# Building half of the float64 weight chunks with one VectorE operation fewer, and sending four more attention tiles through the DMA transpose

## The chip, the cores and the metric

The kernel runs on one core of one Trainium2 chip. The metric is the device time of the one launch in microseconds (us), as the median of three runs. Beside it one execution was recorded by the hardware profiler; its rows are what this text reads.

The engines are called as in the profile: PE (TensorE matmul), PEld (its weight load, which overlaps PE), DVE (VectorE), ACT (ScalarE), POOL (GpSimd) and SP (SyncE, which here only issues DMAs).

## The reference

Clustered attention, then two dense blocks. A query sees only the keys of its own cluster; the cluster is the centroid with the largest normalised product.

```python
q_assign = argmax(einsum('bhsd,hcd->bhsc', q_n, c_n)); k_assign = argmax(... k_n ...)
mask   = q_assign[:, :, :, None] == k_assign[:, :, None, :]
scores = where(mask, D ** -0.5 * q @ k.T, -1e9)
x      = softmax(scores) @ v                       # B=2, H=8, S=768, D=64
h = x @ w_in                                       # 1536 x 512 @ 512 x 2048
g = where(h >= 1, h, where(h <= -1, 0, (h + 1) ** 2 / 4))
x = g @ w_out                                      # 2048 x 512
out = (((x @ w1) * (x @ w2)) @ w3) @ w_out2        # 512 -> 1024 -> 1024 -> 512
```

q, k, v and the centroids are float32. All weights are float64: each arrives as two 32-bit words, and the kernel makes float32 of them on the chip.

## The kernel before

**Attention.** The 2 batches x 4 pairs of heads are 8 units. A unit has 2 groups of 384 queries, a group 6 tiles (2 heads x 3 blocks of 128 queries), so there are 96 tiles `s`, 48 in each batch. A tile goes through: four matmuls into a 128x768 score tile in PSUM (`s_mm`, L853), the row maximum on DVE (L861), a small operation on POOL that turns it into the bias (L866), the exponential on ACT (L874), a transpose, and, when the six tiles of a group are there, the product with v (`pv`, L962 in batch 0, L970 in batch 1).

**The two ways to transpose.** `by_pe(s)` picks one. Where it holds, ACT writes the exponential to SBUF, PE turns it in six 128x128 transposes back into the score tile's PSUM (`s_pT`, L891), and ACT and DVE copy it to `pt`. Where it doesn't, ACT and DVE split the tile into two 16-bit halves in `phl` (L347, L352), and SP issues one DMA transpose from `phl` to `pt` (L921). In batch 0 every tile goes by PE; in batch 1 every sixth, which is 8 of 48.

**Weight chunks.** The float64 weights come in 72 chunks of 128x512 (`chunk`). ACT takes the absolute value of the high word read as a float (L1107); DVE clamps it (L1111, sometimes POOL), shifts its bits left by three (`rebase`, L1117) and puts the two top bits back (`top`, L1123). The low word's upper three bits are then added: in even chunks ACT scales them (L1136) and POOL adds (L1140), in odd chunks DVE shifts and ors (`low`, L1129). Chunks are used at once or stored to DRAM and loaded again.

**Dense blocks.** Weights and activations are split into a high and a low part, and each product is three matmul passes (`mm4`, L1254: 12 matmuls of 384 columns). w3 @ w_out2 is multiplied in advance (`wp_mm`, L1198). Batch 0's dense work runs between the attention tiles of batch 1; batch 1's comes last, most of it in a form with seven products in place of eight (L1507).

**What sets the order.** Nothing is scheduled at run time or while building. All tasks are listed with `add`, and a long string, `ORDER`, names each task and the engine that does it, in the order in which they are issued. Every engine works through its own part of that list in order and waits at each instruction for what it needs. At the start 40 matmuls that compute nothing (`idle_mm`, L463) stand between the first tiles on PE.

Of the kernel before, what the change touches and what calls it, by code (L numbers as in the profile page):

```python
# [8 lines left out]
F32 = mybir.dt.float32  # L9
# [4 lines left out]
U32 = mybir.dt.uint32  # L14
# [24 lines left out]
    "##$V$.$0$4#%#*$X$2#,#0$]#.$Z%s%X%V%Z#(%e#2#4%h%k$6%c$_%y&,%r:m%_$H$8%m$::|$a;.$<%a;<$q%|$c$>%i#_$J&%#i#e$e%u"  # L39
    "&#%]$s#:$@$g$D#Z:o$L$i#o$k:w#N#6:q#>$B$m$##q#c$F#T:s#D;H$N#k&($,:u)u;#$u:y#y%o$()w#|;0#J#H%w#]$o$*$%;%#B)y)|"  # L40
    "#s$P;(;>$R$w*#;X;*#g*%#F$y#P#L;R;,#w$|*($T;2**;g;J;8;4*,*4%#&*;L*.*@;@;6;Z*6;:*B;i*0;q*8*:;k#a*D*L;B#u;u*F;D"
    ";m*<#R;F*2*H;o*>#8;]#@;s*N<(#m*X*Z*J#<*P*R#X#V*u;_*];a;w*_;N;y+(;c*T*V*e;e;P*a*c+4;|;T<**w*m&>&0+6*y*g<6+*<2"
    "+8<B<,*|+,<.+:&3+#+.&9+L<#<R+0+%&7<%*i+2+@<0*k+X+N<e<4<8+<<D+B;V+>*o+D<T+P<F+R<V+Z+F*r+]<u<X+H<H&:<Z+_+T<J+J"
    "+a&G+e+u*s+g&/+V+c,(<g&=,4<L+m,*&4<N<w+w%@<o,6+y,,+|<:,8<i,.<<,@,:<>,#<y<|,<,%<@,0<]<k,L,2<_<P=*,B=:,N,>,D,F"
    ",P=#=%,R&I=(,X<a,H<m<c,u,J<q+i=L,w-4+k&J,Z,y=,<s-6,]=],|+o-8=.=k,_=0=2&N=4,T,W&D-#=6,e=<&T,a-(&Q,g=N=8,c-*-%"
    "=>-,+r=_=|+s-.=a=@&@-:=P=B-@=D-<&B=R-0=F=V=c=T,m&_=H-B=X&Z-2-D>4->=e=g&L&S=i>D&W-L=J=m-F-X=p&c,i-N&k-u&X,l-H"
    "-Z&o=Z&j>R-]=u=q-P-_=s-R-K=w,o-a>#-w>6-T=y>%-V-y>(,q>*-|>,>.-c>8,s%>&e>F>T>H>:>>.(><&].#.*>]-m>V.%.,>X>c>u>Z"
    ">0>J..&b>L-e.0&g>N-g.4>P.@%B>@.6%(-i%%.L-k>_>2.2>B.N?%.B.P.8.:.<-o.D&u&n.F>e>w.H?,.X>z.R>a.Z.J>g?:?J.].>>i._"
# [36 lines left out]
    "[]Zw^.[iZy]u[m^:[k_;[|],]#[(]q]._=^<]%`D^>]0]([*_>^2]*]g^@Z|^6]3_C[,]s^D_6]w_8`F[_]4_G_@^L]e[o^B^H]i]6^R_I]8"
# [54 lines left out]
def cluster_attention_moe_kernel(  # L140
# [947 lines left out]
    def low_by_pool(i):  # L1088
        return i % 2 == 0
# [683 lines left out]
```

## Time and profile before

| | |
|---|---|
| time, median of 3 runs | 726.48 us (725.79 to 728.29) |
| profiled execution | 725.32 us, of it 723.6 us span |
| instructions | 11965 |
| HBM read, written | 73.70 MB, 20.19 MB |

The span runs from the first to the last instruction; the 1.72 us beyond it lie around it. An engine's busy share is a mean over stages that differ: attention of batch 0 up to about 210 us, attention of batch 1 with the dense work of batch 0 up to about 470 us, then dense work alone. The ends of matmuls are modelled, so that short gaps on PE don't show as idle time; the starts of consecutive matmuls tell more.

### The profile page before, as it was taken

The numbers are of one execution on the slowest core, as the hardware profiler recorded it, in microseconds if no ns is written. First come the engines' busy times: TensorE is split into PE (matmuls) and PEld (weight loads), VectorE is DVE, ScalarE is ACT, GpSimd is POOL, SyncE is SP. The second block draws the span as 40 slices with busy tenths as digits, with TensorE's granted clock in tenths as the row PEclk, the third lists the DMA queues.
The fourth block names the chain that finished last, engine by engine and source line by source line (L and its number), as shares of the span: only waits on it lengthen the run. The fifth ranks groups of instructions, "written<-read, shape, count | busy, mean of one in ns | idle before, by whom it ended". The sixth has DMA issues, their size and how long they took to land.

```text
span 723.6 us, 11965 instructions
## 1 busy us (share of the span) xinstructions
PE 704.4 (97%) x4144; PEld 617.9 (85%) x4145; DVE 615.9 (85%) x1134; ACT 465.5 (64%) x870; POOL 285.3 (39%) x358
## 2 busy tenths in 40 slices
PE   5899999999999999999999999999999999999998
PEld 2766666566599999999999999999999999999997
DVE  6998988988987898999999998749987888999851
ACT  7888987766878678788778675425764534454301
POOL 4232325222245343345444525421762432377501
PEclk9999999999999999999999999999999999999999
DMA  8453658656788879888989887854131221122212
GB/s 312 135 193 131 194 192 272 202 191 201 205 166 199 171 175 217 233 235 187 244 217 225 205 230 157 186 164 152 46 103 57 59 88 59 44 72 74 73 52 80
DMA packets 113932, 115.80 MB, mean 160 GB/s; under 512 B 74128, under 2 KB 82768, under 8 KB 113872
## 3 DMA queue, kind: packets, MB, share of 16 engines
q1 hardware_dynamic: 91312, 55.62, 31.8%
q10 hardware_dynamic: 22560, 59.42, 26.6%
q8 instruction: 32, 0.52, 0.3%
q14 instruction: 28, 0.23, 0.1%
HBM read 73.70 MB, written 20.19 MB: 130 GB/s over the span
## 4 chain that ended last, share of the span: by engine, by line
PE 89%; DVE 4%; ACT 3%; DMA 2%; issue 1%; SPq 0%; POOL 0%; ACTq 0%; POOLq 0%; DVEq 0%
PE mo L1254 36%; PE sc L1507 9%; PE sc L853 9%; PE mo L1198 7%; PE mo L1507 5%; PE sc L891 5%; PE sc L1254 5%; PE av L962 4%; PE av L970 3%; PE av L1507 2%; PE av L1254 2%; DMA vn<-phl 1%; DMA kq<-in_qT_dram 1%; DVE nm L861 1%; ACT pt L347 1%
## 5 line engine op out<-in xcount | busy, mean ns | idle before, releaser
L1254 PE MATMUL mo<-X,whl 128*128 128x384 f32 x924 | 169.5, 338 | 0.0
L1254 PEld LDWEIGHTS mo<-X,whl 128*128 128x128 f32 x924 | 159.5, 188 | 2.3 <-issue 0.6
L1254 PE MATMUL mo<-G,whl 128*128 128x384 f32 x732 | 133.2, 337 | 0.0
L1254 PEld LDWEIGHTS mo<-G,whl 128*128 128x128 f32 x732 | 126.6, 188 | 0.9 <-DVE X L352 0.3
L861 DVE TENSOR_REDUCE nm<-sc 128x1 f32<-128x768 f32 x96 | 90.2, 952 | 15.9 <-PE sc L853 13.6
L352 POOL TENSOR_TENSOR whl<-wf,whl 128x512 fp32r<-128x512 f32 x48 | 63.3, 1319 | 73.1 <-ACT whl L347 44.6
L1140 POOL TENSOR_TENSOR wf<-wf,w 128x512 int32<-128x512 int32 x32 | 42.2, 1320 | 80.4 <-DVE wf L1123 32.1
L866 POOL TENSOR_SCALAR nm<-nm 128x1 f32<-128x1 f32 x96 | 26.3, 274 | 102.9 <-DVE nm L861 94.2
L347 ACT ACTIVATE whl<-wf 128x512 fp32r<-128x512 f32 x76 | 47.5, 627 | 29.4 <-PE mo L1254 11.8
L853 PE MATMUL sc<-k,q 128*128 128x512 f32 (+1 forms) x192 | 55.1, 368 | 3.8 <-DVE nm L861 1.6
L1198 PE MATMUL mo<-wo,wf 128*128 128x512 f32 x128 | 58.0, 596 | 0.0
L874 ACT ACTIVATE P<-sc,nm 128x768 f32<-128x768 f32 x56 | 50.1, 898 | 10.6 <-POOL nm L866 5.5
L347 ACT ACTIVATE pt<-sc 128x768 f32<-128x768 f32 (+1 forms) x50 | 39.4, 807 | 18.6 <-PE sc L891 14.7
L853 PE MATMUL sc<-kq 80*128 80x512 f32 (+1 forms) x192 | 49.7, 340 | 0.0
L891 PEld LDWEIGHTS sc<-ident,P 128*128 128x128 f32 x336 | 37.9, 141 | 12.5 <-issue 4.9
L1107 ACT ACTIVATE wf<-w 128x512 f32<-128x512 f32 x64 | 42.4, 672 | 5.7 <-POOL wf L1140 1.7
L891 PE MATMUL sc<-ident,P 128*128 128x128 f32 x336 | 43.9, 275 | 1.6 <-DVE nm L861 1.3
L1123 DVE SCALAR_TENSOR_TENSOR wf<-w,wf 128x512 uint32<-128x512 uint32 x64 | 44.2, 693 | 0.9
L874 ACT ACTIVATE sc<-sc,nm 128x768 f32<-128x768 f32 x40 | 34.7, 868 | 15.5 <-POOL nm L866 15.4
L1198 PEld LDWEIGHTS mo<-wo,wf 128*128 128x128 f32 x128 | 23.3, 190 | 24.5 <-issue 23.7
L352 DVE TENSOR_TENSOR phl<-sc,phl 128x768 f16<-128x768 f32 x40 | 38.1, 952 | 5.6 <-ACT phl L347 5.2
L853 PEld LDWEIGHTS sc<-k,q 128*128 128x128 f32 x192 | 31.4, 189 | 12.2 <-DVE nm L861 3.0
(239 smaller groups left out, 1485.1 us busy)
## 6 DMA issues: line engine op xcount, KB each, us to landing
wf<-wd ACTq DMA_DIRECT2D x64, 256.0 KB, 2.7
w<-in_w_out_dram ACTq DMA_DIRECT2D x24, 512.0 KB, 4.2
wd<-wf SPq DMA_DIRECT2D x48, 256.0 KB, 3.6
w<-in_w3T_dram ACTq DMA_DIRECT2D x16, 512.0 KB, 4.7
w<-in_w_in_dram ACTq DMA_DIRECT2D x16, 512.0 KB, 5.0
w<-in_w_dram ACTq DMA_DIRECT2D x16, 512.0 KB, 4.3
wf<-wp ACTq DMA_DIRECT2D x16, 256.0 KB, 2.9
kq<-in_qT_dram SPq DMA_DIRECT2D x8, 384.0 KB, 3.4
```

Source lines behind the costliest of these rows:

```text
L347: nc.scalar.activation(out=out, in_=in_, func=AF.Copy)
L352: (nc.gpsimd if e == "POOL" else nc.vector).tensor_tensor(out=out, in0=a, in1=b, op=ALU.subtract)
L853: nc.tensor.matmul(ps[:, n], q[0:n_rows, q0:q0 + 128], k[0:n_rows, n], start=first, stop=not first)
L861: nc.vector.tensor_reduce(out=nm, in_=T[("sc", b), s], axis=AX.X, op=ALU.max, negate=True)
L874: nc.scalar.activation(out=new(("P", b), s).rearrange("p n s -> p (n s)") if by_pe(s) else T[("sc", b), s], in_=T[("sc", b), s], func=AF.E ...
L891: nc.tensor.transpose(T[("sc", b), s][:, c], p[:, c], ident)
L1107: nc.scalar.activation(out=T["wf", i], in_=T[w64, i].bitcast(F32)[:, :, 1], func=AF.Abs)
L1123: nc.vector.scalar_tensor_tensor(out=w, in0=T[w64, i][:, :, 1], scalar=0xC0000000, in1=w, op0=ALU.bitwise_and, op1=ALU.bitwise_or)
L1140: nc.gpsimd.tensor_tensor(out=w, in0=w, in1=T[w64, i].bitcast(I32)[:, :, 0], op=ALU.add)
L1198: nc.tensor.matmul(acc, w[:, k4 * 128:(k4 + 1) * 128], wo2[:, hf * 4 + k4], start=(hf == 0 and k4 == 0), stop=(hf == 1 and k4 == 3),)
L1254: nc.tensor.matmul(acc, w[:, a, k4 * 128:(k4 + 1) * 128], rhs(c, k4), start=(first and k4 == 0 and n == 0), stop=(last and k4 == 3 and n = ...
L1507: nc.tensor.matmul(ps, lhs(av, a, k), rhs(bv, c, k), start=k == 0 and n == 0, stop=k == 1 and n == 2,)
```

## The change

`PE_EVERY` goes from (1, 6) to (1, 12): of the 48 tiles of batch 1 now 4 are turned by PE. Tiles 54, 66, 78 and 90 take the way over `phl` and the DMA transpose.

The 36 odd chunks are put together in another way. ACT's absolute value also multiplies by 2^16, which does what `rebase` did by masking; a new ACT operation (`low_floor`) scales the low word and rounds it down to its upper three bits; one DVE operation shifts and ors these in (`shift_low`) and another puts the sign back (`sign`). That is clamp, shift_low, sign in place of clamp, rebase, top, low on DVE, and one ACT operation more. The even chunks stay as they are.

`ORDER` is a new string: all engines' lists change, and some tasks change engine. Counted over the whole program, 44 DMA transposes become 48 and PE has 24 matmuls fewer; DVE has 36 two-operand scalings fewer but 33 copies and casts more and 11 subtractions or additions fewer; ACT has two activations more in all; POOL has 12 additions or subtractions more.

```diff
-    "##$V$.$0$4#%#*$X$2#,#0$]#.$Z%s%X%V%Z#(%e#2#4%h%k$6%c$_%y&,%r:m%_$H$8%m$::|$a;.$<%a;<$q%|$c$>%i#_$J&%#i#e$e%u"
+    "###%$V$.$2$0#*#,#0$X$4$]$Z%s%X%Z#.:m%V#(#2%c#4$6%r%e%k$_$H%|%h:|&#&%$8$:$a%y%_&,#m#L;.%]$<$>$q$c%m$@$J$D$e$F"
...
-    PE_EVERY = (1, 6)
+    PE_EVERY = (1, 12)
...
+        nc.gpsimd.memset(down, -0.4982)
...
+        by_add = low_by_pool(i)
...
-            nc.scalar.activation(out=T["wf", i], in_=T[w64, i].bitcast(F32)[:, :, 1], func=AF.Abs)
+            nc.scalar.activation(out=T["wf", i], in_=T[w64, i].bitcast(F32)[:, :, 1], func=AF.Abs, scale=1.0 if by_add else float(2.0 ** 16))
...
-                out=w, in0=w, scalar1=float(2.0 ** -15), scalar2=float(2.0 ** 16 * 1.875), op0=ALU.max, op1=ALU.min
+                out=w, in0=w, scalar1=float(x * 2.0 ** -15), scalar2=float(x * 2.0 ** 16 * 1.875), op0=ALU.max, op1=ALU.min
+        def low_floor(e):
+            lo = T[w64, i][:, :, 0]
+            nc.scalar.activation(out=lo, in_=lo, func=AF.Identity, scale=float(2.0 ** -29 - 2.0 ** -41), bias=down)
+
+        def shift_low(e):
+            w = T["wf", i].bitcast(U32)
+            nc.vector.scalar_tensor_tensor(
+                out=w, in0=w, scalar=3, in1=T[w64, i][:, :, 0], op0=ALU.logical_shift_left, op1=ALU.bitwise_or
+            )
+
+        def sign(e):
+            w = T["wf", i].bitcast(U32)
+            nc.vector.scalar_tensor_tensor(
+                out=w, in0=T[w64, i][:, :, 1], scalar=0x80000000, in1=w, op0=ALU.bitwise_and, op1=ALU.bitwise_or
             )
...
-        def low(e):
-            w = T["wf", i].bitcast(U32)
-            nc.vector.scalar_tensor_tensor(
-                out=w, in0=T[w64, i][:, :, 0], scalar=29, in1=w,
-                op0=ALU.logical_shift_right, op1=ALU.bitwise_or,
-            )
...
-                add(("wc", i, 3), {"DVE": 0.6}, t - 7.0, low, [("wc", i, 2)], frees=[(w64, i)])
+                add(("wr", i), {"ACT": 0.56}, t - 8.5, low_floor, [("wl", i), "c_const"])
+                add(("wc", i, 2), {"DVE": 0.6}, t - 7.8, shift_low, [("wc", i, 0), ("wr", i)])
+                add(("wc", i, 3), {"DVE": 0.6}, t - 7.0, sign, [("wc", i, 2)], frees=[(w64, i)])
```

**Place 1: PE around tile 54,** the first tile of batch 1 that changes its way. `sc` rows with `k,q` and `kq` are the four matmuls of one tile's scores, `whl` rows are twelve matmuls of the dense block, `ident,P` the six transposes. Before:

```order
L1254 MATMUL mo_123<-X_75,whl 128x384 x12
L853 MATMUL sc_1736<-k_97,q_100 128x512
L853 MATMUL sc_1736<-k_97,q_100 128x256
L853 MATMUL sc_1736<-kq_103 128x512
L853 MATMUL sc_1736<-kq_103 128x256
L1254 MATMUL mo_1730<-X_75,whl 128x384 x12
L891 MATMUL sc_1735<-ident,P_106 128x128 x6
L1254 MATMUL mo_1731<-X_75,whl 128x384 x12
```

And now:

```order
L1268 MATMUL mo_124<-X_75,whl 128x384 x12
L855 MATMUL sc_1736<-k_98,q_101 128x512
L855 MATMUL sc_1736<-k_98,q_101 128x256
L855 MATMUL sc_1736<-kq_104 128x512
L855 MATMUL sc_1736<-kq_104 128x256
L1268 MATMUL mo_1730<-X_75,whl 128x384 x12
L1268 MATMUL mo_1731<-X_75,whl 128x384 x12
```

The six transposes are gone and the dense products on both sides follow each other; the same happens at tiles 66, 78 and 90. The rest of PE's list keeps its pattern, with neighbours exchanged here and there.

**Place 2: DVE at the first odd chunk.** `wo` is the chunk's float32, `w` its two words; `phl` rows belong to the cluster masks. Before:

```order
L1111 TENSOR_SCALAR wo_118<-wo_118 128x512
L567 STREAM_TRANSPOSE phl_109<-phl_109 128x384
L1117 TENSOR_SCALAR wo_118<-wo_118 128x512
L562 TENSOR_TENSOR phl_110<-P_107,amx 128x384
L1123 SCALAR_TENSOR_TENSOR wo_118<-w_112,wo_118 128x512
L567 STREAM_TRANSPOSE phl_110<-phl_110 128x384
L1129 SCALAR_TENSOR_TENSOR wo_118<-w_112,wo_118 128x512
```

And now:

```order
L564 TENSOR_TENSOR phl_111<-P_108,amx 128x384
L569 STREAM_TRANSPOSE phl_110<-phl_110 128x384
L1114 TENSOR_SCALAR wo_119<-wo_119 128x512
L569 STREAM_TRANSPOSE phl_111<-phl_111 128x384
L1124 SCALAR_TENSOR_TENSOR wo_119<-wo_119,w_113 128x512
L1130 SCALAR_TENSOR_TENSOR wo_119<-w_113,wo_119 128x512
```

Four rows of the chunk became three: the short one (L1117) is gone, the two long ones stay as long ones, and the mask's rows moved ahead of the chunk.

**Place 3: PE in its first 20 us.** `kq,cT` rows are the products with the centroids, four for each half of k or q; `ident` into `av` are matmuls that compute nothing; `raw` is the transpose of v; `tri` the cluster masks. Before:

```order
L533 MATMUL sc_178<-kq_117,cT 32x384 x8
L463 MATMUL av<-ident 128x128 x3
L783 MATMUL sc_177<-ident,raw_91 128x128 x6
L463 MATMUL av<-ident 128x128
L574 LDWEIGHTS tri
L574 MATMUL sc_177<-phl_109,tri 128x384
```

And now:

```order
L535 MATMUL sc_179<-kq_118,cT 32x384 x4
L465 MATMUL av<-ident 128x128 x2
L535 MATMUL sc_179<-kq_118,cT 32x384 x4
L576 LDWEIGHTS tri
L576 MATMUL sc_178<-phl_110,tri 128x384
L465 MATMUL av<-ident 128x128 x4
L785 MATMUL sc_178<-ident,raw_92 128x128 x6
```

The first mask product moved ahead of v's transpose, and two of the idle matmuls went between the two halves of the centroid products. There are 40 idle matmuls in both programs, all ahead of tile 6.

## Rows read from the trace of the kernel before

**Rows 1.** The page's busy time by engine: us, share of span, instructions.
```profile
PE 704.4 (97%) x4144; PEld 617.9 (85%) x4145; DVE 615.9 (85%) x1134; ACT 465.5 (64%) x870; POOL 285.3 (39%) x358
```

**Rows 2.** Busy time by stage: length, then us and count by engine.
```profile
core 0: us, PE busy (x) PEld busy (x) DVE busy (x) ACT busy (x) POOL busy (x), PEclk, DMA share, GB/s
0.00:15.00 15.00, 6.81 (x36) 1.69 (x37) 8.56 (x25) 12.75 (x16) 8.20 (x15) 1.00 0.85 306
15.00:30.00 15.00, 12.16 (x93) 10.86 (x92) 13.75 (x29) 10.84 (x18) 2.54 (x4) 1.00 0.58 190
30.00:42.00 12.00, 9.97 (x70) 8.56 (x68) 10.79 (x21) 10.48 (x20) 4.27 (x7) 1.00 0.34 112
42.00:60.00 18.00, 17.75 (x103) 11.42 (x103) 17.21 (x29) 15.88 (x28) 4.97 (x11) 1.00 0.50 173
60.00:210.00 150.00, 149.01 (x778) 94.16 (x776) 132.54 (x217) 116.61 (x200) 48.51 (x72) 1.00 0.64 201
210.00:450.00 240.00, 238.53 (x1509) 223.89 (x1508) 220.35 (x381) 181.01 (x334) 103.35 (x122) 1.00 0.89 208
450.00:690.00 240.00, 240.00 (x1395) 237.47 (x1394) 202.66 (x419) 114.53 (x252) 109.58 (x128) 1.00 0.32 91
690.00:723.60 33.60, 30.16 (x174) 29.84 (x173) 10.00 (x19) 3.41 (x7) 3.89 (x3) 1.00 0.18 63
```

**Rows 3.** PE in order of time around a transposed tile: start, us, what.
```profile
225.15 0.82 PE L891 MATMUL sc<-ident,P 128*128 128x128 f32 x6
225.73 2.35 PE L1254 MATMUL mo<-X,whl 128*128 128x384 f32 x12
227.92 0.57 PE L853 MATMUL sc<-k,q 128*128 128x512 f32 x2
...
228.67 2.25 PE L1254 MATMUL mo<-G,whl 128*128 128x384 f32 x12
230.76 0.51 PE L1254 MATMUL mo<-X,whl 128*128 128x384 f32 x2
```

**Rows 4.** DVE and ACT groups of the chunks: busy us, mean ns.
```profile
L1117 DVE TENSOR_SCALAR wf<-wf 128x512 uint32<-128x512 uint32 x64 | 28.6, 452 | 0.8
L1123 DVE SCALAR_TENSOR_TENSOR wf<-w,wf 128x512 uint32<-128x512 uint32 x64 | 44.2, 693 | 0.9
L1129 DVE SCALAR_TENSOR_TENSOR wf<-w,wf 128x512 uint32<-128x512 uint32 x32 | 23.5, 735 | 0.6
L1136 ACT ACTIVATE w<-w 128x512 uint32<-128x512 uint32 x36 | 24.3, 674 | 1.5 <-POOL wf L1140 1.1 <-DMA w<-in_w3T_dram 0.4
```

**Rows 5.** ACT over 384 columns from PSUM, with and without a pointer bias.
```profile
L1262 ACT ACTIVATE tmp<-mo,half 128x384 f32<-128x384 f32 x32 | 18.4, 574 | 7.4 <-PE mo L1254 7.2
L347 ACT ACTIVATE tmp<-mo 128x384 f32<-128x384 f32 x24 | 11.6, 487 | 38.6 <-PE mo L1254 37.2 <-DVE whl L352 0.9 <-DVE wf L1129 0.4
```

**Rows 6.** What PE waited for: us in total, times, longest.
```profile
PE av L439 <- DVE P L435: 5.8, 1, 5.8
PE sc L533 <- DMA kq<-in_qT_dram: 1.9, 2, 1.4
PE sc L853 <- DVE nm L861: 1.6, 2, 1.1
PE sc L853 <- DVE phl L352: 1.5, 2, 0.8
```

**Rows 7.** PE in order of time, where it waited for ACT at 41 us.
```profile
41.34 0.62 PE L853 MATMUL sc<-k,q 128*128 128x256 f32 x2 [0.24 <-ACT pt L347]
```

**Rows 8.** Transposes of group 4,1 on SP, its product on PE; transposes' landing.
```profile
247.81 3.66 SPq L921 DMA_TRANSPOSE pt<-phl  x2
...
260.46 3.12 PE L970 MATMUL av<-pt,vn 128*64 128x384 f16 x36
...
DMA to landing us min/median/max: 3.6/5.2/10.2
```

More of the change, by code (lines that the diff above doesn't have):

```diff
@@ L44 @@
[L44 to L48, printed above, removed]
@@ L94 @@
[L94 to L95 removed]
+    "###%$V$.$2$0#*#,#0$X$4$]$Z%s%X%Z#.:m%V#(#2%c#4$6%r%e%k$_$H%|%h:|&#&%$8$:$a%y%_&,#m#L;.%]$<$>$q$c%m$@$J$D$e$F"
+    "%a#6#a#e#P;<%u:o$s$g#Z$i$B$L$k#F;H%i:q%o$m:s)u$N:w:u%w#:$#:y#V#H#8;#;()w#g#c$o$u#_#i#@#X;0#y)y)|;8#u#w$w#B*#"
+    "#q;X*%$P;%#>$y$|;*;,;2;R;>$R$T*(**#R#o;g#]*4*,%#&*;B;4*.;_&)$,#T;6;@;:*6;J*@*B#s$%;Z*0;i*8#N*:;L;N*L#|;k*D*F"
@@ new lines @@
+    "*<;D#k;m*2;F*>*H#<;]#J#D*N;u;q*X;o*P*J$($**Z;a*R*]*u<(*_+(*T;P;T;w;c;e*a*W;|*c*e*g+4*w<6*m<*;s<B+*<2&0*y+6+,"
+    "*|&5&3<R&>+.;y<,+8+:<.<#+L+#<8<%+0<<+<+%<:&7*i+2+@<0*k<D+X+B<4;V<T+N<e+D<X*o+P+F+Z+R*r+]&/+_+H+T*s+>&=+J+V+u"
+    "+a+e<V<><F<H+c,4&:<Z,(+w&8<g+m,*+y<u<o<@,,+|,6<i<J,8,:,#<],.<k<_,L<L<N<m,&=*&F<|,0,<,@+g<P,B=:<q<w,N,2,P<y,>"
+    "=#=%,D,R,X&H=L<b,F<c,u,w=,=(+i+k%>=.,Z,H,T=]%%<s,]%(,y=0=4=2=@=6,_,|,a,K,W=V-#+o=<=N=>=B-4&c=Q-(+r-%=k,c=8-*"
+    "-,-6&D=c=|=_+s-8-:=D=a=e-.=R&U-@&@&B=F-0-<=g=i=I,e&L,m-2-B-D=J&N-?&K,g-F,i&R&Y=u=T&W>(=m-H-X,l=X,o=o-L-K&P&_"
@@ new lines @@
+    "-N-P-Z=Z>4>D>R-R-],r=q=s&e-_&^-u=w>>%B>#-w-T-a&b-y>c-V>%=y>J>*-|.#,s>6-d>,>8>F>T>.-e.(>]-g>:-m.*>u.%&k>H.,>L"
+    "..>N>V>X><>0&g-i&[>2>@.4%*>P.@-l.L.6%@?,>Z.8>i.0>B.B.D.:.N>_.2&n&r.P&i.F.<.R&u-o>e?%.X.Z.H>a>w.]?:>y>|._&p?#"
+    "?(-q.J?J.>>q.T.V>g>k>m>s.u.a?2/4.w?.>o/(&y?0?*?]/6.c.y.|&|/*(%()?m/,&w/@/#/./0($(-?P?D-s?<?4%,.m%D/B?>?L?_?@"
+    "/8/:/<?a?6.e?8.g?N?R/%%./2?T/>?c?V?B%F%0?o?s?|%2?g/D?F?H/F/H@2?q%4(*?e%H?i%J?X/L?u/J?Z.i/N/X@D.k&s%L/P?k@,/Z"
+    "/R/T%6/]?w%N@#/_?y@T(.@&.o.r%8/a/V/c%P.s@c@8%:@(/u@*@4/m%<%R%T@.@F@V@s/w/y/e(4@6@:@N0(@<04@H/|0#@JA,@>0608@Z"
@@ new lines @@
+    "0@@L@00*0:0,@P0&0B0.000D@m0<@A/g/i0F0LA<0H@X@]@e03@_0X/k@g@a@B0N@R0>@i0P0J0Z/o@kAJ0R0]0u@yA60T0w@u@o@qA.@w0y"
+    "A>@|0|/r0_AB0a0WA#A%A@ALAD0cAFAH(01(/s(20eA0AZ1#1L0g1*0m1,1.10ANAP1NA2AT1%ARAVA4A(A*(612A81416180iF4FP1@Aa0l"
+    "1X(81:1PA:1Z1B1]1_1D0o(;1<(=1FA]1H1RAmA_AX(>Ac1J(EAe(BAg1>(A1e1g(M(H1TAi0q1a1W(NAk1i1c2*(GAo0sB21kAq1u2,(J1m"
+    "BP1w2.201y1|(P(Z22(RB424B61o2#2%1r1s26(T2(Bo(VAsAuAw(X282:BRBTB%B(Ay2F(]B82<2H2JC42>2A2LBc2BB+B,B:A|B=2DBr2N"
+    "BDB#2PCRCqBeB>2RBg2TB/B1C7F>BsC(C9BFBiFkB@BH2cBB2V2XBV2eBJ2g2ZC*BM2]2_C-BuBk2iBNCU2aBm2kC.BXCV3%3(2mBZBw3*D%"
@@ L96 @@
+    "e(fBeifDe*e%g@f|f?e]fHeQe_gigke,emg$g*g.g%eqf6fJfPeog2esg(gNgmekeuewfWg4fLeygpfNfZf]fFgqg0h4g6g8g:h_f_gyfRfX"
+    "gthae|gFgBh#g~h&fcg-gvgxfTh)fgfih*fegDfahBfkhghihcfmfoh8hFgPiTh6h<gHfqh,heh0hogRhsg<hkh2gTgXi*huhDg]h:gVhmiW"
+    "gJi,h.h>hHiXi_g`gahwi8iqh~gZi#i.hNi:hzh@hJi2iagci<isicgfi]i%hLhqggi0hPi|i>ivhRi4hTj4hXh[i)iwi@iDhViHiJiZi6iL"
+    "j>iBh]iFiNiyj$iQieiRikj&j(igjPiij6jAj9imjCj.j0j2jSjUj<jVj:jJjXjZjLj*j,j^j`iojNjDjgjjjGjkjHjajcje"
 )
@@ L194, in cluster_attention_moe_kernel @@
     nbig = const.tile([128, 1], F32, name="nbig")
+    down = const.tile([128, 1], F32, name="down")
     wp = dram.tile([DM // 128, 128, KF2, 128], F32, name="wp")
@@ L1162, in chunk @@
             add(("wc", i, 0), {"DVE": 0.34, "POOL": (1.92, LATE)}, t - 8.6, clamp, [("wabs", i)])
-            add(("wc", i, 1), {"DVE": 0.34}, t - 8.2, rebase, [("wc", i, 0)])
-            add(("wc", i, 2), {"DVE": 0.6}, t - 7.8, top, [("wc", i, 1)])
-            if low_by_pool(i):
+            if by_add:
+                add(("wc", i, 1), {"DVE": 0.34}, t - 8.2, rebase, [("wc", i, 0)])
+                add(("wc", i, 2), {"DVE": 0.6}, t - 7.8, top, [("wc", i, 1)])
                 add(("wr", i), {"ACT": 0.56}, t - 8.5, low_round, [("wl", i)])
```

89 lines of the change are left out of this document (37 added, 52 removed).

## The prediction

> **What bounds the kernel now.** I read the busy time by engine first, then the busy time by stage, then what PE waited for. PE is busy 704.4 us of 723.6, DVE 615.9 [rows 1]. By stage the picture is sharper [rows 2]. Up to 42 us PE stands idle for 8.19, 2.84 and 2.03 us in the three stretches, 13.06 in all; from 42 to 690 us it is idle for 0.25 + 0.99 + 1.47 + 0 = 2.71; in the last stretch, which ends with the last copy and store, for 3.44. So from 42 us on the time is the length of PE's own list. DVE is the next, 220.35 of 240 us between 210 and 450, but PE hardly waits for it: the list of PE's waits has eleven rows, the largest are the first centroid transpose (5.8) and the first loads (1.9), and the waits for the row maximum and for the 16-bit low half are 1.6 and 1.5 [rows 6]. A change pays here if it shortens PE's list or one of the waits up to 42 us, and it costs if it puts a wait into the stretch after that. The granted clock is 1.00 in every stage, so no term of it is in the sum.
>
> **Four tiles leave PE.** What one costs PE is read from the starts around one of them [rows 3]. From the first of its six transposes (225.15) over the twelve dense matmuls behind it to the next instruction (227.92) are 2.77 us; twelve dense matmuls without transposes in front take 230.76 - 228.67 = 2.09. One tile is 0.68 us, four are 2.72. It comes from the stage between 210 and 450 us, where PE is 99.4% busy and dense products stand on both sides of the gap, ready to close it, as the first place in the order shows. I count it in full: -2.72.
>
> The same tiles get what the other 40 of batch 1 have. ACT and DVE make their two halves as before (into `phl`, not `pt`), which is no new operation on either. SP gets four DMA transposes; two take it 3.66 us, one 1.83 [rows 8]. SP is in order, so the stores and loads behind wait that much longer. The transpose itself lands after 5.2 us (median; 3.6 to 10.2), and then the product of the group may start. For the group that holds tile 54 the last two transposes are issued from 247.81 on, the second from about 249.64, and the product starts at 260.46, 10.8 us later [rows 8]. A sixth transpose ahead of it leaves 9.0 us, still over the median landing. From below the cost is 0, from above it is what a landing beyond 9.0 us takes from PE (10.2 would be 1.2). I take 0, since the median is far inside.
>
> The Trainium skill (VectorE: DVE Perf Modes, "The three transpose paths" and "Rules for kernel authors") speaks against this: it gives 390 ns for a 128x128 transpose on TensorE and 1309 ns by DMA, and advises TensorE where the result may lie in PSUM. By its figures six blocks cost 2.3 us on one and 7.9 us on the other (an estimate from that page), so four tiles would lose 22 us if somebody waited for them. The rows show 0.68 us for the one, 5.2 for the other, and nobody waiting for the 5.2; by them the rule holds for the latency and not for the engine that sets the end.
>
> **Chunks on DVE and ACT.** Each of the 36 odd chunks loses one DVE operation, the short one: 0.452 us [rows 4], 16.3 in all. The two that stay long are bounded by the two rows of the same form, 0.693 and 0.735; the sum over both is the same as before, so 0 for them. ACT gets 36 operations. The even chunks' scaling has 0.674 us; the new one has a pointer bias, which in another ACT form makes 574 of 487 ns, 87 more [rows 5]; so 0.674 to 0.761 each, and I take the upper, 27.4 us. ACT has that room: it is busy 10.84 of 15, 10.48 of 12, 15.88 of 18, 116.61 of 150 and 181.01 of 240 us [rows 2], 100 us idle up to 450. It doesn't get them in full anyway: the new order gives DVE 33 copies and casts that ACT had, and POOL 12 subtractions that DVE had. The freed DVE time is mostly spent on that.
>
> What is it worth on PE? After 42 us at most the 2.71 us that PE idles there; and since DVE's list has hardly become shorter I take nothing of it. Before 42 us the order lets me bound it. Ahead of the ninth tile's maximum, three rebases (chunks 1, 3, 5) are gone on DVE, 1.36 us, and one tile's copy came in that ACT had; ahead of the sixth tile's copy ACT has three new operations, 2.28 us. ACT is idle for 4.16 + 1.52 us between 15 and 42 [rows 2], which hides them if they fall into its gaps; at 41 us PE waited 0.24 us for ACT [rows 7], so the cover there is thin. So the start is between -1.4 (DVE's gain in full) and +2.3 (ACT's load in full). I take 0, between the two. The mask product that moved ahead on PE (third place) can't start before DVE has made its input, and v's transpose behind it loses nothing; 0.
>
> **Sum.** -2.72 on the profiled execution's 725.32 is 722.60. The median of the runs is 726.48, 1.16 above it, so the forecast in the terms of the median is 723.76, that is 723.8 us: -0.37%.
>
> **Rivals.**
> 1. *The start gets shorter too.* DVE's 1.36 us and the earlier mask reach PE, and some of the 2.71 us of idle time go: -2.72 - 2 = 721.8. For it: DVE is busy 13.75 of 15 and 10.79 of 12 us there, and PE waits for it. Against: the order fills DVE again.
> 2. *The start gives it back.* The three new ACT operations ahead of the first product delay the copies that PE waits for, by 2.28 us, and nothing after 42 us can catch up, since PE has no slack there: -2.72 + 2.28 = -0.44, 726.0. For it: the wait at 41 us. Against: ACT's 5.7 us of gaps.
> 3. *A transpose comes late, slower than before.* Between 210 and 450 us the DMA engines are busy to 0.89 [rows 2]. If one more transpose in that crowd makes the longest landing longer by a median one, 10.2 + 5.2 = 15.4 us, the product of tile 54's group waits 15.4 - 9.0 = 6.4 us; PE is in order, and all that stands behind waits with it: -2.72 + 6.4 = +3.7, 730.2. It decides from a landing of 9.0 us on, and is slower than before by more than the bound from 13.9 on. That is what the rule of the Trainium skill on transposes (VectorE: DVE Perf Modes, "Rules for kernel authors") would come to in this kernel. Against it: PE waited for no product in the trace, with 40 tiles on that way.
> 4. *The new order alone.* With every list changed, waits may appear anywhere. I give it no own time; it widens the forecast's own range to about 1.3 us on either side.
>
> **How the numbers follow.** The forecast gets 0.52, the first rival 0.19, the second 0.20, the third 0.09. A measurement of this kernel can tell about 0.3% from no change, 2.2 us, so faster is below 724.3 and slower above 728.7. Of the forecast's 0.52 about seven in ten lie below 724.3, 0.37, and the rest within; the first rival is faster, the second within, the third slower. Faster 0.37 + 0.19 = 0.56, same 0.15 + 0.20 = 0.35, slower 0.09. The range takes in the first rival down to -2.72 - 1.4 - 1.5 = 720.9 and the second with the upper bounds of start and landing together, -2.72 + 2.28 + 1.2 = 727.2; it leaves out the third and the ends of the others. The forecast's own range is 722.5 to 725.1.
>
> **What would show it.** PE's busy time falls by about 2.7 us, with 24 transposes fewer. PE's idle time up to 42 us stays near 13 us and after it near 2.7. DVE's group of the masked shift has half its count. The new ACT group has 36 entries of 0.67 to 0.77 us. No row of PE's waits names a product. It would be wrong if PE's waits grow by more than 2 us anywhere, first of all for ACT's copies before 42 us, or if a product waits for a transpose.

## The result, and the profile after

The changed kernel takes 732.61 us (median of 16 runs, 728.30 to 734.91); the kernel before took 725.84 in the same comparison (16 runs, 724.35 to 729.39). The ratio is 1.0083 with a 95% interval of 1.0064 to 1.0101: about 6.1 us slower (4.6 to 7.3), where 2.7 us less were forecast. The time lies outside the forecast's range.

The profiled execution took 729.0 us, 727.3 of it span. It is one of the faster of its runs: its mean granted clock is 1.000, while 10 of the other 15 had 0.995 or less. What these have more is seen in a second trace below.

The page of the changed kernel, busy time by engine as in [rows 1]:

```profile
PE 706.3 (97%) x4120; PEld 620.5 (85%) x4121; DVE 620.3 (85%) x1120; ACT 467.9 (64%) x872; POOL 308.2 (42%) x371
```

PE has the 24 instructions fewer, and is busy 1.9 us longer. DVE has not become shorter (615.9 before), as the prediction said: the new order fills it again.

Busy time by stage, columns as in [rows 2]:

```profile
0.00:15.00 15.00, 6.21 (x37) 2.38 (x37) 10.03 (x23) 11.80 (x15) 7.36 (x16) 1.00 0.85 306
15.00:30.00 15.00, 11.65 (x89) 10.26 (x86) 14.16 (x28) 11.28 (x19) 3.44 (x4) 1.00 0.56 190
30.00:42.00 12.00, 10.22 (x72) 8.73 (x70) 11.00 (x20) 10.99 (x21) 4.60 (x6) 1.00 0.36 114
42.00:60.00 18.00, 17.92 (x101) 11.84 (x103) 17.22 (x32) 16.59 (x29) 4.57 (x9) 1.00 0.41 141
60.00:210.00 150.00, 147.96 (x774) 92.81 (x772) 133.00 (x211) 115.80 (x202) 56.18 (x74) 1.00 0.66 211
210.00:450.00 240.00, 238.49 (x1485) 223.57 (x1484) 218.13 (x369) 184.78 (x339) 113.08 (x126) 1.00 0.89 206
450.00:690.00 240.00, 239.96 (x1385) 237.38 (x1384) 204.32 (x421) 112.44 (x245) 119.00 (x137) 1.00 0.32 93
690.00:727.30 37.30, 33.85 (x192) 33.53 (x190) 12.49 (x25) 4.20 (x9) 0.00 (x0) 1.00 0.21 71
```

PE is idle 13.92 us up to 42 us (13.06 before) and 3.67 from 42 to 690 (2.71 before). That is 1.8 us of the 3.7 by which the two profiled spans differ. The rest hides in rows that look full: between 450 and 690 us PE is busy for all of the 240 us in both kernels, with 1395 instructions before and 1385 now. The same list takes longer there.

The durations of the chunks' operations are near what [rows 4] and [rows 5] gave. The rows that answer to them (`L1120` is the new ACT operation, `L1124` and `L1130` are the two that stay on DVE):

```profile
L1120 ACT ACTIVATE w<-w,down 128x512 uint32<-128x512 uint32 x36 | 27.7, 770 | 3.4 <-POOL wf L1152 2.3 <-ACT P L876 0.6 <-issue 0.5
L1130 DVE SCALAR_TENSOR_TENSOR wf<-w,wf 128x512 uint32<-128x512 uint32 x32 | 23.2, 725 | 0.4
L1124 DVE SCALAR_TENSOR_TENSOR wf<-wf,w 128x512 uint32<-128x512 uint32 x32 | 23.2, 724 | 0.9
```

What PE waited for, columns as in [rows 6]:

```profile
PE av L441 <- DVE P L437: 7.4, 1, 7.4
...
PE mo L1268 <- DVE X L353: 0.8, 1, 0.8
PE mo L950 <- DVE wf L350: 0.7, 1, 0.7
```

The first row was 5.8. The other two weren't in the list of before. No row names a product.

### The profile page after: what moved, and what is told of

Read it like the earlier page. It is cut to its first block, busy times and chain, and to the rows that moved or that the text cites. A ratio compares the mean times of both kernels' runs of the same rounds, so it can differ in the third digit from the quotient of the medians.

```text
span 727.3 us, 11952 instructions
## 1 busy us (share of the span) xinstructions
PE 706.3 (97%) x4120; PEld 620.5 (85%) x4121; DVE 620.3 (85%) x1120; ACT 467.9 (64%) x872; POOL 308.2 (42%) x371
## 4 chain that ended last, share of the span: by engine, by line
PE 86%; DVE 5%; DMA 4%; ACT 3%; issue 2%; POOL 0%; ACTq 0%; POOLq 0%; DVEq 0%
PE mo L1268 34%; PE sc L1521 9%; PE sc L855 8%; PE mo L1212 6%; PE sc L1268 6%; PE mo L1521 6%; PE sc L893 4%; PE av L964 4%; PE av L972 3%; PE av L1521 2%; PE av L1268 2%; DMA vn<-phl 1%; DMA pt<-phl 1%; DMA wd<-wf 1%; DVE nm L863 1%
## 5 line engine op out<-in xcount | busy, mean ns | idle before, releaser
L1268 PE MATMUL mo<-G,whl 128*128 128x384 f32 x696 | 129.1, 340 | 0.8 <-DVE X L353 0.8
L1268 PEld LDWEIGHTS mo<-G,whl 128*128 128x128 f32 x696 | 122.3, 188 | 2.8 <-DVE X L353 1.1
L1152 POOL TENSOR_TENSOR wf<-wf,w 128x512 int32<-128x512 int32 x32 | 45.0, 1408 | 56.9 <-DVE wf L1142 18.1
L868 POOL TENSOR_SCALAR nm<-nm 128x1 f32<-128x1 f32 x96 | 29.7, 310 | 92.0 <-DVE nm L863 88.7
L348 ACT ACTIVATE whl<-wf 128x512 fp32r<-128x512 f32 x71 | 44.6, 628 | 29.0 <-PE mo L1268 10.0
L876 ACT ACTIVATE sc<-sc,nm 128x768 f32<-128x768 f32 x44 | 38.3, 870 | 26.4 <-POOL nm L868 25.3
L876 ACT ACTIVATE P<-sc,nm 128x768 f32<-128x768 f32 x52 | 46.4, 896 | 13.0 <-DVE nm L863 7.0
L353 DVE TENSOR_TENSOR phl<-sc,phl 128x768 f16<-128x768 f32 x44 | 41.8, 951 | 8.2 <-ACT phl L348 7.9
L353 POOL TENSOR_TENSOR wh<-ws,wh 128x256 fp32r<-128x256 f32 x42 | 31.3, 758 | 17.8 <-DVE wh L350 9.6
L348 ACT ACTIVATE pt<-sc 128x768 f32<-128x768 f32 (+1 forms) x40 | 31.8, 811 | 9.7 <-PE sc L893 7.4
```

The source lines that it names most:

```text
L348: nc.scalar.activation(out=out, in_=in_, func=AF.Copy)
L353: (nc.gpsimd if e == "POOL" else nc.vector).tensor_tensor(out=out, in0=a, in1=b, op=ALU.subtract)
L868: nc.gpsimd.tensor_scalar(out=tl[s, "nm"], in0=tl[s, "nm"], scalar1=SCALE, scalar2=EC, op0=ALU.mult, op1=ALU.add)
L876: nc.scalar.activation(out=new(("P", b), s).rearrange("p n s -> p (n s)") if by_pe(s) else T[("sc", b), s], in_=T[("sc", b), s], func=AF.E ...
L1152: nc.gpsimd.tensor_tensor(out=w, in0=w, in1=T[w64, i].bitcast(I32)[:, :, 0], op=ALU.add)
L1268: nc.tensor.matmul(acc, w[:, a, k4 * 128:(k4 + 1) * 128], rhs(c, k4), start=(first and k4 == 0 and n == 0), stop=(last and k4 == 3 and n = ...
```

## The experiments

Each group of runs was made on one chip, beside runs of the kernel before on that chip; between groups the ratios are compared. "No shift" means that the new constant lies in a second column of the constant 0.5, so that no other tile in SBUF moves.

### 1. The changed kernel again, and three neighbours

**The changed kernel once more.** No edit.

> The changed kernel once more, as the measure for the three beside it, and for a second trace. Both theories expect the 1.008 of the first comparison again, some 6 us over before. Theory 'clock': if a part of the loss is PE at half clock, the mean granted clock of this trace is below 1.00 (the first comparison listed 0.995 for most runs, which over 730 us is about 7 us at half clock, 3.6 us lost), and a window of the trace shows where. Theory 'no clock': the trace reads 1.00 like the first, and the time still is near 732.

732.86 us, ratio 1.0103 (1.0067 to 1.0139). This trace has the lower clock, and shows where. Two stretches of it, columns as in [rows 2]:

```profile
354.00:366.00 12.00, 11.26 (x64) 10.85 (x63) 8.29 (x20) 7.97 (x16) 6.71 (x7) 1.00 1.22 142
366.00:374.00 8.00, 6.23 (x26) 5.87 (x27) 7.39 (x14) 5.83 (x12) 1.65 (x3) 0.79 0.95 251
```

PE stands idle at about 366 us, and then runs at 1.2 GHz for a part of the next stretch: a mean of 0.79 over 8 us is 3.4 us at that half clock. No other stretch ahead of the last us has it. The place was there in the first trace too, with 0.83 us of idle time and no fall of the clock. Theory "clock" holds, and the wait at 366 us comes first.

**No shift.**

```diff
-    half = const.tile([128, 1], F32, name="half")
-    down = const.tile([128, 1], F32, name="down")
+    hd = const.tile([128, 2], F32, name="half")
+    half, down = hd[:, 0:1], hd[:, 1:2]
```

> Changed kernel, but the new constant -0.4982 lies in a second column of the constant that holds 0.5, so that no tile in SBUF moves against the kernel before. Theory 'place': the new 32-byte constant moved the moving operands of the dense products (G, one X, Yp) by 32 bytes, and that is why the excess over the usual pitch of the dense matmuls went from 4.9 to 9.5 us; then 4 to 5 us come back here, ratio to before about 1.002, and the mean start-to-start of 384-column matmuls between 490 and 690 us falls from 176.1 to 175.0 ns. Theory 'order': the place does nothing, 1.008 as in the changed kernel, pitch 176.

730.44 us, ratio 1.0051 (1.0032 to 1.0071). The 1.0103 of its neighbour falls by 0.5%, 3.8 us; the mean time from start to start of the dense matmuls whose moving operand is `G`, after 470 us and over starts at most 200 ns apart, falls from 176.6 ns to 173.7, as before the change (173.7). Theory "place" holds. The other half of the loss stays.

**The kernel before with the unused constant.**

```diff
+    down = const.tile([128, 1], F32, name="down")
...
+        nc.gpsimd.memset(down, -0.4982)
```

> Kernel before with nothing but the unused 32-byte constant added, so that every tile behind it lies where it lies in the changed kernel. Theory 'place': 4 to 5 us slower than before (ratio 1.006), pitch of the dense matmuls 176 ns. Theory 'order': same as before within 0.3%, pitch 175.

729.98 us, ratio 1.0053 (1.0033 to 1.0072), 3.8 us. On `G` 176.7 ns. Nothing was computed that was not computed before: 32 bytes of an unused tile cost more than the whole change was to gain. The same row of PE in time, 36 dense matmuls on `G`, in the kernel before:

```profile
359.11 6.41 PE L1254 MATMUL mo<-G,whl 128*128 128x384 f32 x36
```

and in this one, where they take 0.11 us longer:

```profile
360.98 6.52 PE L1256 MATMUL mo<-G,whl 128*128 128x384 f32 x36
```

The tile called `X` in the rows tells moved from unmoved within one trace. Ahead of 345 us it is `X0`, which the program lays out ahead of the new constant; from 390 to 470 it is `X1`, which lies behind it. 24 matmuls on each, in the kernel before:

```profile
215.28 4.34 PE L1254 MATMUL mo<-X,whl 128*128 128x384 f32 x24
...
436.87 4.33 PE L1254 MATMUL mo<-X,whl 128*128 128x384 f32 x24
```

and in this one, where those on `X0` take the same and those on `X1` 0.08 us longer:

```profile
216.73 4.34 PE L1256 MATMUL mo<-X,whl 128*128 128x384 f32 x24
...
439.57 4.41 PE L1256 MATMUL mo<-X,whl 128*128 128x384 f32 x24
```

Summed over the dense matmuls on `G`, `X` and `BX` from 210 us on, the longer times make 4.3 us, enough for the 3.8.

**Both parts in the order of before,** no shift.

```diff
  the tasks of ORDER by name, every odd chunk i and every tile s of 54, 66, 78, 90
-  (wc, i, 1) DVE          -  (spT, s) PE   (shi, s) ACT   (sT, s) DVE
+  (wr, i) ACT             +  (shi, s) ACT   (slo, s) DVE   (sT, s) DMA
```

> Both parts of the change (three VectorE operations and the new ScalarE operation in odd chunks, every twelfth tile by TensorE) issued in the order of the kernel before: the new ScalarE operation stands where the short VectorE operation stood, the four tiles' second half and transpose where their last copy stood. Addresses as before. Theory 'the parts pay, the order loses': 725.8 - 2.7 = 723.1, ratio 0.996. Theory 'the parts themselves cost': slower than before by what ScalarE's 36 operations delay, 1.00 to 1.008. The trace's waits of PE up to 42 us and at the products of the four tiles tell where.

733.91 us, ratio 1.0110 (1.0083 to 1.0138). The first theory falls: the loss isn't the new order's alone. PE waits 3.3 us in three places for DVE's `phl`; in the trace without shift it is 4.3, of it 3.6 at 366 us. This trace also has 10.2 us at 1.2 GHz ahead of 42 us (a mean of 0.88), and its first product is 2.5 us later than in the kernel before; not all of its loss need be the edit's.

### 2. Which part

**The wait at 366 us.** In the trace without shift all that leads to it can be read. Rows in order of time, all engines; ACTq and SPq are issues of DMAs:

```profile
353.84 2.23 SPq L774 DMA_TRANSPOSE vn<-phl  x1
...
354.39 0.36 ACTq L1101 DMA_DIRECT2D w<-in_w_dram  x1
354.72 0.80 ACT L348 ACTIVATE phl<-sc 128x768 f16<-128x768 f32 x1
...
356.62 5.79 SPq L923 DMA_TRANSPOSE pt<-phl  x1
...
366.37 0.81 ACT L348 ACTIVATE phl<-sc 128x768 f16<-128x768 f32 x1 [5.61 <-DMA vn<-phl]
...
367.22 0.96 DVE L353 TENSOR_TENSOR phl<-sc,phl 128x768 f16<-128x768 f32 x1 [5.44 <-ACT phl L348]
...
368.23 1.01 PE L855 MATMUL sc<-k,q 128*128 128x512 f32 x2 [3.60 <-DVE phl L353]
```

Batch 1 has two `phl` buffers. v's transpose of the unit (353.84) reads one, tile 78's (356.62) the other: that is the tile that PE turned before. Tile 77 comes behind both. Its high half (366.37) needs a `phl` buffer and waits 5.61 us until v's transpose has landed. DVE's low half follows (367.22), and only then is tile 77's score buffer free, one of two, which PE needs for the scores after the next. The time to landing in this stretch (last column), of the kernel before:

```profile
vn<-phl SPq DMA_TRANSPOSE x1, 6.0
```

and in the run without shift:

```profile
w<-in_w_dram ACTq DMA_DIRECT2D x2, 512.0 KB, 8.0
...
pt<-phl SPq DMA_TRANSPOSE x2, 7.7
vn<-phl SPq DMA_TRANSPOSE x1, 12.4
```

So two things met: a third user for two buffers, and transfers that took twice their time. During the wait the clock fell:

```profile
354.00:366.00 12.00, 10.62 (x62) 10.21 (x60) 7.74 (x18) 6.62 (x14) 6.68 (x7) 1.00 1.18 131
366.00:374.00 8.00, 5.62 (x17) 5.03 (x18) 5.90 (x10) 5.45 (x10) 1.65 (x3) 0.57 0.81 202
```

**Tile 78 on PE again,** no shift, new order.

```diff
-        return s % PE_EVERY[s // NU] == 0
+        return s % PE_EVERY[s // NU] == 0 or s in (78,)
```

Tile 78's own tasks stand in `ORDER` where a tile that PE turns has them.

> Changed kernel without the shift of addresses, and tile 78 alone turned by PE again (three tiles of batch 1 leave PE, not four; new order otherwise). Theory 'buffer': the new way of tile 78 costs, since v's transpose of the same unit and tile 78's take both phl buffers between 354 and 367 us, so that ACT's half of tile 77 waits for v's transpose (5.6 us) and PE 1 to 3.6 us for that tile's score buffer, after which the clock falls to half for up to 6.8 us. Then here PE has no idle time at 366 us, the clock stays at 1.00 there, and the time falls by 3 to 6 us against the run with all four tiles (730.4), less 0.68 for the transposes: 725 to 728. Rival 'DVE': DVE is late there anyway; then the wait at 366 us stays and the time is 731.

725.08 us, ratio 0.9984 (0.9971 to 0.9997). Against 1.0051 that is 0.67%, 4.9 us, although PE got 0.68 us of transposes back: the way of this one tile cost about 5.5 us. Of the 5.7 us between the spans of the two traces 5.3 are won at this place. PE doesn't stop at 366 us, and the clock stays:

```profile
354.00:366.00 12.00, 11.76 (x70) 11.28 (x69) 10.65 (x23) 9.04 (x18) 6.90 (x8) 1.00 0.70 162
366.00:374.00 8.00, 8.00 (x47) 7.58 (x46) 7.75 (x15) 6.94 (x13) 2.78 (x3) 1.00 0.90 236
```

All 12 runs have a mean clock of 0.997 or more; 5 of the 8 with tile 78 on the other way had 0.995. Theory "buffer" holds, "DVE" falls.

**ACT's second table first,** no shift, all four tiles moved.

```diff
  ACT's tasks in ORDER
-  c_sqrt   (qh, 0, 0)   c_exp
+  c_sqrt   c_exp   (qh, 0, 0)
```

> Changed kernel without the shift of addresses; ACT loads the second table before it copies the first half of q, as before (one task moved by two places). Theory 'collision': POOL's subtraction then starts later, DVE's scaling of the centroids takes 0.42 us a pair as before and not 2.0, PE's first instruction comes at 5.8 us and not at 7.4; but the first tile's products at 42 us gain at most the 1.1 us that the start had lost. 729.5 to 730.4. Rival 'no matter': PE's first instruction comes at 5.8 us and the products at 43.3 all the same, 730.4.

731.93 us, ratio 1.0080 (1.0058 to 1.0102). What this edit removes, in the first trace of the changed kernel:

```profile
5.32 1.97 DVE L437 TENSOR_SCALAR P<-P,rr 128x64 f32<-128x64 f32 x2
...
5.40 1.83 POOL L353 TENSOR_TENSOR q<-kq,kq 64x768 fp32r<-64x768 f32 x1 [3.02 <-ACT kq L348]
...
7.43 0.44 PE L441 MATMUL av<-ident,P 128*128 128x128 f32 x1 [7.43 <-DVE P L437]
```

In the kernel before DVE's pair took 0.42 us, ahead of POOL's subtraction (5.85); here it took 1.97, beside it: its second operation started at 5.49, behind POOL's 5.40, and ended at 7.29, just behind POOL's 7.23. The Trainium skill (SBUF — State Buffer, "Who interferes with whom") says that VectorE and GpSimd share a pair of SBUF ports as an exclusive lock, that this operation can use it, and that the one that issues later is blocked; the two rows agree. With the edit PE starts at 5.82 and not at 7.35, and the first product comes at 42.41 us instead of 43.31. PE came earlier to 366 us and waited 4.2 us there, not 3.6; the span of the trace is 0.6 us shorter, the median 0.3% longer, and the two intervals overlap. So the collision is shown, and a gain from its removal is not. The other traces leave little room for one. Where the two collide, in five traces, PE starts at 7.2 to 7.4 us and the first product comes at 42.8 to 43.4. With this edit, in five others, PE starts at 5.7 to 5.9 and the product comes at 42.4 to 42.8, once at 44.15. In two traces of the unedited start (those shifted by 32 and 64 bytes, below) the pair happened to come ahead of POOL; the product came at 43.09 and 44.26.

**The four tiles alone,** in the order of before.

```diff
-    PE_EVERY = (1, 6)
+    PE_EVERY = (1, 12)
```

> Kernel before with only the four tiles changed to the DMA transpose, everything else in the order of before. Theory 'buffer': phl's two buffers are taken by v's transpose and one tile's, so that PE waits where a changed tile stands beside v's transpose (the first tile of each second group): 727 to 731, with the waits near 291 and 342 to 367 us that the run with both parts in the old order showed. Theory 'forecast': 0.68 us for each of four tiles, 727.3 - 2.7 = 724.6.

727.38 us, ratio 1.0020 (1.0001 to 1.0039). Between the two: no gain of 2.7, no loss of 3. The trace has the lower clock long before the first of the four tiles:

```profile
30.00:42.00 12.00, 10.26 (x56) 9.61 (x57) 9.12 (x17) 8.52 (x17) 3.61 (x6) 0.72 0.27 88
```

In the kernel before the clock is 1.00 there [rows 2]. Up to this place the two kernels have the same list, and PE has the same two waits around it (1.12 us up to 28 and 1.34 up to 31; 1.12 and 1.33 before). The fall puts PE back by 2.2 us in this execution. So the clock can fall with no edit to cause it, and a median can hold some of that: 4 of the 23 executions of the kernel before beside this one have a mean clock of 0.995 or less. In this order it is a product that waits for its transpose, the place that the third rival named:

```profile
376.21 3.09 PE L970 MATMUL av<-pt,vn 128*64 128x384 f16 x35 [1.36 <-DMA pt<-phl]
```

**The chunks alone,** in the order of before, no shift.

> Kernel before with only the 36 odd chunks changed (three VectorE operations, one more on ScalarE, which stands where the short VectorE operation stood), in the order of before, addresses as before. Theory 'no worth': DVE is not on the path after 42 us, so within 0.3% of before. Rival 'ScalarE': 36 x 0.67 = 24 us more on ScalarE delay the exponentials, most of all at the start, where the run with both parts had its products at 44.7 us instead of 42.2: 729 to 732.

735.28 us, ratio 1.0127 (1.0101 to 1.0154), the worst of all. DVE is busy 604.4 us, 11.5 less, and ACT 488.3, 22.8 more; PE's first product is 1.35 us late (with a granted clock of 0.86 between 30 and 42 us, so that this isn't ACT's alone), and PE's largest waits later are these:

```profile
PE sc L855 <- DVE phl L353: 2.2, 2, 1.9
...
PE mo L1268 <- DVE tmp L1293: 1.4, 1, 1.4
```

Ahead of the longer one (341.98) DVE itself waits for ACT's new operation:

```profile
338.67 0.69 DVE L1124 SCALAR_TENSOR_TENSOR wf<-wf,w 128x512 uint32<-128x512 uint32 x1 [1.77 <-ACT w L1120]
```

So DVE's 11.5 us are worth nothing on PE, and ACT's 22.8 delay it in this order, where no other work leaves ACT. The new order moves such work, and in it the chunks alone cost less (1.0040, in part 4, where ACT's second table comes first as well); it is a needed part of the change.

### 3. What makes the transfers slow, and the place

**One weight load later,** no shift, all four tiles moved.

```diff
  ACT's tasks in ORDER
-  (wl, 74)   (hr, 0, 15, 1)   (hs, 0, 15, 1) ... (whi, 70)   (shi, 77)
+  (hr, 0, 15, 1)   (hs, 0, 15, 1) ... (wl, 74)   (whi, 70)   (shi, 77)
```

> Changed kernel without the shift of addresses, all four tiles by DMA transpose, and one weight load (chunk 74's, 512 KB) issued behind ACT's operations of the next 6 us instead of 0.5 us behind v's transpose at 354 us. Theory 'crowd': v's transpose took 12.45 us there, and the load beside it 11.7, because a load and a second transpose came while it was in flight; without that load v's transpose lands after 6 to 7 us, tile 77's half finds its phl buffer free by 361 us, PE's wait at 366 us is gone, the clock stays up, and the time is 725 to 726. Rival 'two transposes': tile 78's transpose behind v's is enough; v's still lands after 9 us or more, PE waits over 1 us, 728 to 730.

726.20 us, ratio 0.9997 (0.9976 to 1.0017). v's transpose lands in 4.6 us with tile 78's still behind it:

```profile
pt<-phl SPq DMA_TRANSPOSE x2, 5.5
vn<-phl SPq DMA_TRANSPOSE x1, 4.6
```

Theory "crowd" holds: the load issued 0.5 us behind v's transpose made both slow. It isn't a law. Of the 795 transposes in the traces of this study 58 had a weight load issued within 1 us behind them; they landed after 6.2 us in the median, 5.0 to 13.0, while the 348 with no weight load issued within 4 us of them took 4.0. PE is left with another wait at the same place, for DVE's sum in the dense block:

```profile
366.90 6.75 PE L1268 MATMUL mo<-G,whl 128*128 128x384 f32 x36 [1.74 <-DVE X L353]
```

**Three tiles, no shift, ACT's second table first.**

> Tile 78 on PE (three tiles moved), no shift of addresses, and ACT's second table load ahead of the first copy of q. Theory 'swallowed': the 0.9 us that this start gained at 42 us in the run with four tiles was lost in the wait at 366 us; with that wait gone it reaches the end: 725.1 - 0.9 = 724.2, ratio 0.997. Rival 'no matter': later waits take it all the same, 725.1.

724.28 us, ratio 0.9969 (0.9952 to 0.9987): the shortest time here. Against 0.9984 that is 1.1 us less, and the two intervals overlap. The traces don't show the start in it: PE starts 1.6 us earlier than in the run with tile 78 on PE, but the first product comes at 42.83 us (42.78 there), and the 1.2 us by which the span is shorter are mostly two waits of PE, 0.61 us at 162 and 0.41 at 250, that this execution doesn't have. The page's first line has PE at 98%:

```profile
PE 704.3 (98%) x4127; PEld 616.5 (85%) x4127; DVE 619.0 (86%) x1120; ACT 468.3 (65%) x872; POOL 308.7 (43%) x371
```

**The place, twice more,** with three tiles moved: the constant as an own tile of 32 bytes, and of 64.

```diff
-    half, down = hd[:, 0:1], hd[:, 1:2]
+    down = const.tile([128, 1], F32, name="down")
...
+    down = const.tile([128, 16], F32, name="down")[:, 0:1]
```

> Tile 78 on PE, and the new constant in a tile of its own again, so that G, one X and Yp lie 32 bytes further (72160, 109024, 133600: multiples of 32, not of 64). Theory 'place': 3 to 4 us slower than the 725.1 without the shift, 728 to 729, the pitch of the dense matmuls up over all of 450 to 720 us. Rival: the shift cost only in the run with the kernel before by chance, 725.

> The same with a 64-byte constant tile: G, X and Yp lie 64 bytes further (72192, 109056, 133632: multiples of 64 again). Theory 'alignment to 64': 725.1 as without the shift. Rival 'any shift': 728 to 729 as with 32 bytes (the places relative to X0, whl and the other tiles that did not move decide).

728.79 us, 1.0027 (1.0010 to 1.0044), and 728.10, 1.0018 (0.9999 to 1.0037), against 0.9984 without a shift. The pitch (start to start, counted as above) after 470 us on `G`, which moved, is 173.7 ns without, 176.6 and 176.1 with a shift; on `BX`, which did not move, 175.1, 174.0 and 174.8. Only the matmuls whose operand moved are slower. Alignment to 64 bytes isn't the rule.

### 4. What was still open

**All four back on PE,** no shift, ACT's second table first: chunks and order alone.

> New order, new chunks, ACT's second table first, no shift of addresses, and all four tiles turned by PE as in the kernel before (8 of 48 in batch 1). What is left of the change is the chunks and the order. Forecast's term (-0.68 us for each tile that leaves PE, nothing for the chunks): the run with three tiles moved had 724.28, so 724.28 + 2.04 = 726.3 here, no different from before (725.9). Rival 'the transposes were free on PE': 724.3 again. Rival 'chunks pay': below 725.

728.41 us, ratio 1.0040 (1.0025 to 1.0054). The span of its profiled execution is 724.1 us, 1.9 above the 722.2 of the kernel with three tiles, where 2.04 were expected; PE's busy time differs by 1.5 (705.8 to 704.3). Lined up by PE's list, the two traces part by 0.7, 0.9 and 0.7 us near 225, 285 and 430 us, where the three tiles stand. But the medians differ by 0.7%, 5 us. The profiled execution took 725.92 us; the longest of the 11, 729.92, has a mean clock of 1.00 as well, and what it waits for no trace shows. In these two traces three tiles gain 1.5 to 1.9 us; where the other 3 us of the medians come from is open. By the medians the chunks and the new order alone cost 2.9 us, which the expectation had at next to nothing.

**A shift by 128 bytes,** three tiles, ACT's second table first.

> Three tiles moved, ACT's second table first, the constant in a tile of 128 bytes, so that G, X and Yp lie 128 bytes further. Without a shift this kernel takes 724.28; 32 bytes cost 3.7 us and 64 cost 3.0 in its sister. Theory 'place within 128 bytes': 724.3 again, pitch on G 173.6 ns. Rival 'any shift against what stands still': 727 to 728, pitch on G 176 to 177 ns.

727.05 us, ratio 1.0021 (1.0007 to 1.0035), against 0.9969 without; on `G` 174.7 ns after 470 us and 174.6 before. The theory of the place within 128 bytes falls as well, though the pitch is nearer to the old one than with 32. It makes 2.0 us over all dense matmuls, near the 2.1 by which the spans of the two traces differ and half of the 3.8 between the ratios. Which places are good was not found.

**All four tiles, the late load, ACT's second table first.**

> All four tiles by DMA transpose, no shift, ACT's second table first, chunk 74's load issued late: every repair at once. The late load alone gave 726.2 with PE idle 1.7 us at 366.9 us for the sum of the dense block (DVE X). Theory 'DVE bounds 366 us': the 0.9 us of the start is lost in that wait, which grows to 2.5, and the time stays 726. Rival: it is 725.3, or 724.28 - 0.68 = 723.6 if the wait goes too.

726.20 us, ratio 1.0005 (0.9987 to 1.0023). The time stays, as "DVE bounds 366 us" expected, but its reason is not shown: the wait at 366 us is 1.9 us (1.7 without the start, 2.5 expected), and in this trace the first product comes at 44.15 us, 0.8 later than without. The profiled execution took 729.65 us, 3.5 above the median, and the clock fell behind this wait (a mean of 0.79 from 366 to 374 us), so it can't say what the median does. With all repairs four tiles are still slower than three (1.0005 against 0.9969).

## Why the prediction was wrong

**The step that failed** is the landing of the transposes: "From below the cost is 0, from above it is what a landing beyond 9.0 us takes from PE (10.2 would be 1.2). I take 0, since the median is far inside." It was worked out for tile 54 [rows 8], and for one reader of the transposes, the product. The text notes that the halves now go "into `phl`, not `pt`" and gives this no cost. Tile 78 was not looked at, nor the two `phl` buffers that it shares with its neighbours and with v's transpose. There ACT, DVE and PE wait behind each other, PE for 3.6 us in the run without shift (0.8 to 4.2 in the others), and in three of these four traces the clock falls. Taking this one tile back gives about 5.5 us, and issuing the load later 3.9 (1.0051 to 0.9997) with all four tiles moved. The third rival had the mechanism, a late transpose in the crowd of [rows 2], and its size (6.4), with a chance of 0.09; it looked for it at the product, where it came up only in the run of the four tiles alone (1.36 us).

**The clock.** "The granted clock is 1.00 in every stage, so no term of it is in the sum": true for one trace, and a new wait made a term of it. In the run without shift the granted clock is 0.57 over the 8 us from 366: 6.9 us at 1.2 GHz. PE runs for 5.6 of the 8 us, so about 2.8 us are lost behind the 3.6 of the wait. The wait is not all of it: 1.7 us of waiting (and 0.8 behind it) came with a fall in the second trace of the changed kernel and 1.7 with none in the run with the late load, and in the traces of four tiles alone, of both parts in the order of before and of the chunks alone the clock fell at 30 us. What decides that is open.

**A term that the sum didn't have** is the constant of 32 bytes: 3.1 to 3.8 us in three pairs of kernels. The prediction took an unwritten 0 for it. Nothing in the profile of before could have priced it, but that the constant moves `G`, `X1` and `Yp`, which are laid out behind it, could be read from the program.

**The start** was taken as 0 between -1.4 and +2.3. The first product came 0.75 us later in the first trace, but also 1.0 us later in the kernel before with the unused constant, whose list is the old one. One copy of ACT ahead of a table load, which the text didn't see, brought POOL's subtraction over DVE's scaling; that this sets the first product is not shown.

**What held:** a tile on PE is worth its 0.68 us in two traces (1.9 of 2.04 us for three, by the spans; the medians say 5); the new ACT operation takes 770 ns (761 taken); the chunks are worth nothing on PE. In the order of before they take 11.5 us from DVE and give 22.8 to ACT, where 16.3 and 27.4 were counted, and that load costs, as the second rival had it, but mostly later than 42 us.

**The sum by what was measured,** in parts of 725.8 us: -2.7 for four tiles, +5.5 for tile 78's wait with the clock, +3.1 to 3.8 for the place: +5.9 to 6.6. Measured are 6.1 (4.6 to 7.3) in the first comparison and 7.5 (4.9 to 10.1) in the second. That the sum comes out is no proof of it, since its two larger terms are differences between runs on the way from the one kernel to the other. The start is left open, and so are the 2.9 us that the chunks and the order cost by the medians, against three tiles worth 5 us where 2 were counted.

## What to carry to other kernels

When work goes from an engine to a queue, list every buffer that it takes on the way, and for each moved piece the neighbours in the ring at that place; the piece that meets a third user decides, not the median one. An idle time on PE of a few us can cost nearly as much again by the clock behind it (2.8 us behind 3.6), and a part of what is gained ahead of it is lost in it. Give a new small constant a place that moves nothing, or measure the kernel with the empty constant first.

## What was not expected of the hardware

- Dense matmuls of 384 columns take 173.7 or 176.6 ns from start to start, depending on where in SBUF their moving operand lies; 32, 64 and 128 bytes further gave 176.6, 176.1 and 174.7. No rule was found.
- A transpose and a 512 KB load issued 0.5 us behind it took 12.4 and 11.7 us together, and 4.6 us for the transpose once the load came 4.5 us behind.
- DVE's pair of 128x64 scalings took 1.97 us beside a POOL subtraction and 0.42 without.
- With the same list and the same waits of 1.1 and 1.3 us the granted clock at 30 us fell to 1.2 GHz in one execution and not in another; the fall cost 2.2 us.
